# Small tail copies and differences moved from VectorE to ScalarE and GpSimd in a fused attention and gated-MLP kernel

## The chip, the cores and the metric

The kernel runs on one core of one Trainium2 chip. The metric is the device time of one execution in microseconds (us). The core has five engines that work side by side, each through its own queue in order: TensorE (PE, matrix products and transposes), VectorE (DVE), ScalarE (ACT), GpSimd (POOL) and SyncE (SP, which issues most DMAs).

## The reference

Decayed causal attention with 8 batches, 8 heads, a sequence of 576 and a head size of 64, followed by a gated MLP that mixes along the sequence. All inputs and outputs are float32.

```python
scores = scale * q @ k.T                    # per batch and head, 576 x 576
decay  = cum[..., :, None] - cum[..., None, :]   # cum: running sum of log(clip(f))
attn   = softmax(where(causal, -1e9, scores + decay))
x      = (attn @ v)                         # heads side by side: [8, 576, 512]

h      = maximum(x @ w_in, 0.0)             # 512 -> 1024
u, v   = h[..., :512], h[..., 512:]
v_n    = (v - mean(v)) / sqrt(var(v) + 1e-06)
v_s    = einsum('ts,bsd->btd', w_spatial, v_n) + b_spatial[None, :, None]
out    = (u * v_s) @ w_out                  # 512 -> 512
```

## The kernel before, in words

*Arithmetic.* Most matrix products are made from split numbers: a float32 value a is rounded to a shorter format (`hi`, a copy into a tile of type F32R) and the rest is kept as `lo = a - hi`. A product is then the sum of hi x hi, hi x lo and lo x hi. So nearly every operand costs a rounding copy and a difference on the smaller engines before PE can use it. The first pairs of heads (`P < NQ`, `P < NF`) go in plain float32.

*Tiles.* The sequence of 576 is four blocks of 128 and a tail of 64. The tail is what makes the code uneven: a tile with 64 rows or columns leaves half of an engine's 128 partitions empty, so two tails are put together where that is possible.

*Attention.* There are 32 pairs of heads, four to a batch. For each pair `attention` makes transposed probabilities (`transposes`, evicted from PSUM by `evac`: ACT's copy to `eh` at L309, DVE's difference to `el` at L310), the next pair's scores (`scores`: DVE's pass L264 out of PSUM, ACT's exponential L266, POOL's normalisation L274), and the products with v (`attend`: ACT's copy to `xh` at L368, DVE's passes to `xl` at L369 and L371). At the end of a pair, L411 copies the 64 tail columns of `xl` to columns 576 to 639 of `xh`, so that one later product handles the tail's hi and lo together.

*The MLP.* `moe(b)` works on one batch. It makes v for five sequence tiles (four of 128 and the tail), takes statistics (L452, L453, L454, L455), normalises (L456), rounds to `th` (named vnh, ACT, L458), and takes the difference (POOL, L460). For the tail tile, L463 copies the rounded value also into `vb_` (named vb), and L464 writes the difference to partitions 64 to 127 of `th`; both run on DVE. Then it makes u (evicted at L479), and, in two halves of the sequence (256 and 320 columns), the spatial sums; L501 multiplies them by u in place (`g`), L504 rounds `g` to `gh`, and L505 takes the difference `gl`. In the second half the last 64 columns are the tail: L508 copies them from `gh` and `gl` to `gt`, which collects the tails of two batches, so that one `w_out_tile` of 128 rows serves both. `w_out_tile` multiplies by w_out and stores the result. L529 evicts the product to `o` and L531 issues the store.

*Buffers.* PSUM holds two score buffers, two for transposes, two for the MLP, and one each for x0 and x1. The tag U has nine buffers, which hold the eight u tiles and the gl tiles in turn; `gh` has the tag GH, vnh five buffers of its own.

*Order.* `attention` and `moe` are generators that are stepped alternately, by rough PE times (`yield` values), so that attention runs a batch and a quarter ahead of the MLP. In what order the instructions of one engine are finally issued is set by a planner at build time, which simulates a timeline with a cost model (`schedule_with_timeline_sim=True`) and picks ready instructions. At run time each engine follows its list in order and waits on semaphores. The weights are decoded from 64-bit floats on chip at the start (L141 to L151), which loads DVE, ACT and POOL in the first 140 us.

Of the kernel before, what the change touches and what calls it, by code (L numbers as in the profile page):

```python
# [13 lines left out]
ALU = mybir.AluOpType  # L14
# [8 lines left out]
S = 576  # L23
D = 64
NB = 4
TL = 512
# [7 lines left out]
def f32(ap):  # L34
    return ap.bitcast(F32)
# [3 lines left out]
def attn_gmlp_kernel(ctx: ExitStack, tc: tile.TileContext, qk, v, f, w_in, w_sp, b_sp, w_out, out):  # L39
# [17 lines left out]
    V, A, G, T, SY = nc.vector, nc.scalar, nc.gpsimd, nc.tensor, nc.sync  # L57
# [35 lines left out]
    def decay_rows():  # L93
        ft = wk.tile([64, S], F32, name="ft", tag="vt")
        SY.dma_start(out=ft, in_=f)
        ones = wk.tile([64, S], F32, name="ones", tag="xl", bufs=5)
        V.memset(ones, 1.0)
        r0 = cst.tile([64, 2, QK], F32, name="r0", tag="el")
        decay_consts(r0[:], 1)
        V.tensor_scalar(out=ft, in0=ft, scalar1=1.0e-4, scalar2=1.0, op0=ALU.max, op1=ALU.min)  # L100
        A.activation(ft, ft, AF.Ln)
        A.activation(lnc[0:1, 2:3], ft[0:1, 0:1], AF.Exp)
        V.tensor_tensor_scan(out=r0[:, 0, 640:QK], data0=ones, data1=ft, initial=0.0, op0=ALU.mult, op1=ALU.add)
        queries_rows(r0[:], 1, V.tensor_copy, A.copy)
        return r0
# [88 lines left out]
    vb_ = cst.tile([66, DM], F32R, name="vb")  # L194
    G.memset(f32(vb_[64:66, :]), 1.0)

    def mm(o, l, r, st, sp):
        T.matmul(o, l, r, start=st, stop=sp)  # L198
# [177 lines left out]
    def attention(b, ws=None):  # L376
        for P in range(b * PPB, (b + 1) * PPB):
            if P == 0:
                r0s.append(decay_rows())
                for h in range(2):  # L380
                    prep(0, h)

                warm = ps_a.tile([128, 512], F32, name="x0")
                for _ in range(26):
                    mm(warm, zm[:, 0:128], zm[:, 0:512], True, True)
                split_rows(ws, r0s[0])
                split(1)
                yield from scores(0, 0)
                yield from scores_tail(0)
                yield from scores(0, 1)  # L390
            nxt = P + 1 < NPAIR
            prep_v(P)
            if nxt:
                prep(P + 1, 0)
                prep(P + 1, 1)
            yield from transposes(P, 0)
            if nxt:
                yield from scores(P + 1, 0)
            yield from transposes_tail(P)
            if P + 2 < NPAIR:  # L400
                split(P + 2)
            if nxt:
                yield from scores_tail(P + 1)
            xh = wk.tile([128, 640], F32R, name="xh", tag="xh", bufs=5)
            xl = wk.tile([128, S], F32R, name="xl", tag="xl", bufs=5)
            yield from attend(P, 0, xh, xl)
            yield from transposes(P, 1)
            if nxt:
                yield from scores(P + 1, 1)
            yield from attend(P, 1, xh, xl)  # L410
            V.tensor_copy(xh[:, S:640], f32(xl[:, TL:S]))  # L411
            xs[P] = (xh, xl)

    gt = {}
# [9 lines left out]
    def moe(b):  # L424
        X = [xs.pop(b * PPB + p) for p in range(PPB)]
        vh, vl = [], []
        for i in range(NB + 1):
            ps = acc(b)
            n = 0
            for p in range(PPB):  # L430
                xh, xl = X[p]
                if i < NB:
                    t = slice(128 * i, 128 * i + 128)
                    terms = ((xh[:, t], winh), (xh[:, t], winl), (xl[:, t], winh))
                else:
                    terms = ((xh[:, TL:640], winh), (xh[:, TL:640], winl))
                for l, r in terms:
                    mm(ps, l, r[:, p, DM:2 * DM], n == 0, n == len(terms) * PPB - 1)
                    n += 1
                yield 648  # L440
            th = mo.tile([128, DM], F32R, name="vnh", tag="vnh", bufs=5)
            tlo = mo.tile([128, DM], F32R, name="vnl", tag="vnl", bufs=4) if i < NB else None
            x = mo.tile([128, DM], F32, name="vx", tag="vx", bufs=2)
            st = mo.tile([128, 6], F32, name="st", tag="st", bufs=2)
            mv = mo.tile([128, 2], F32, name="mv", tag="mv", bufs=2)
            m = slice(0, 128)
            if i == NB:
                m = slice(0, 64)
                A.copy(x[64:128, :], ps[64:128, :])
                V.tensor_tensor(out=x[m, :], in0=ps[m, :], in1=x[64:128, :], op=ALU.add)  # L450
            A.activation(x[m, :], ps if i < NB else x[m, :], AF.Relu)
            V.bn_stats(out=st[m, :], in_=x[m, :])  # L452
            V.bn_aggr(out=mv[m, :], in_=st[m, :])  # L453
            G.tensor_tensor(out=mv[m, 1:2], in0=mv[m, 1:2], in1=lnc[m, 0:1], op=ALU.add)  # L454
            G.tensor_tensor(out=mv[m, 1:2], in0=mv[m, 1:2], in1=lnc[m, 1:2], op=ALU.pow)  # L455
            V.tensor_scalar(out=x[m, :], in0=x[m, :], scalar1=mv[m, 0:1], scalar2=mv[m, 1:2],  # L456
                            op0=ALU.subtract, op1=ALU.mult)
            A.copy(th[m, :], x[m, :])  # L458
            if i < NB:
                G.tensor_tensor(out=tlo, in0=x, in1=f32(th[:]), op=ALU.subtract)  # L460
                vl.append(tlo)
            else:
                V.tensor_copy(vb_[m, :], f32(th[m, :]))  # L463
                V.tensor_tensor(out=th[64:128, :], in0=x[m, :], in1=f32(th[m, :]), op=ALU.subtract)  # L464
            vh.append(th)
            yield 0
        us = {}
        for j in range(NJ):
            for t0, nt in HALVES:
                ps = acc(b)  # L470
                n = 0
                for p in range(PPB):
                    xh, xl = X[p]
                    for l, r in ((winh, xh), (winl, xh), (winh, xl)):
                        mm(ps[:, 0:nt], l[:, p, 128 * j:128 * j + 128], r[:, t0:t0 + nt], n == 0, n == 3 * PPB - 1)
                        n += 1
                    yield 369
                us[j, t0] = mo.tile([128, 320], F32, name="u", tag="U", bufs=9)
                A.activation(us[j, t0][:, 0:nt], ps[:, 0:nt], AF.Relu)  # L479
        if b == 0:  # L480
            for n in range(8):
                load_rest(n, wo_v, woh, wol, 'GH', 3)
        if b % 2 == 0:
            gt[0] = [mo.tile([128, NJ, 128], F32R, name=f"gt{r}", tag=f"gt{r}") for r in range(2)]
        r0 = 64 * (b % 2)
        for t0, nt in HALVES:
            gh, gl = [], []
            for j in range(NJ):
                ps = acc(b)
                o = ps[:, 0:nt]  # L490
                js = slice(128 * j, 128 * j + 128)
                for c in range(NB):
                    mm(o, vh[c][:, js], sph[:, c, t0:t0 + nt], c == 0, False)
                    mm(o, vh[c][:, js], spl[:, c, t0:t0 + nt], False, False)
                    mm(o, vl[c][:, js], sph[:, c, t0:t0 + nt], False, False)
                    yield 370
                mm(o, vh[NB][:, js], spta[:, t0:t0 + nt], False, False)
                mm(o, vb_[:, js], sptb[:, t0:t0 + nt], False, True)
                yield 246
                g = us[j, t0][:, 0:nt]  # L500
                V.tensor_tensor(out=g, in0=o, in1=g, op=ALU.mult)  # L501
                gh.append(mo.tile([128, 320], F32R, name="gh", tag="GH", bufs=3))
                gl.append(mo.tile([128, 320], F32R, name="gl", tag="U", bufs=9))
                A.copy(gh[j][:, 0:nt], g)  # L504
                G.tensor_tensor(out=gl[j][:, 0:nt], in0=g, in1=f32(gh[j][:, 0:nt]), op=ALU.subtract)  # L505
                if t0:
                    for r, gg in enumerate((gh[j], gl[j])):
                        V.tensor_copy(gt[0][r][:, j, r0:r0 + 64], f32(gg[:, 256:320]))  # L508
            for c0 in (0, 128):
                yield from w_out_tile(b, [g[:, c0:c0 + 128] for g in gh], [g[:, c0:c0 + 128] for g in gl],  # L510
                                      [(b, t0 + c0, 0, 128)])
        if b % 2 == 1:
            yield from w_out_tile(b, *[[g[:, j, :] for j in range(NJ)] for g in gt[0]],
                                  [(b - 1, TL, 0, 64), (b, TL, 64, 64)])
# [98 lines left out]
```

## Time and profile before

| | |
|---|---|
| median of 3 runs | 826.72 us (823.64 to 827.42) |
| the profiled execution | 826.3 us, span 824.5 us |
| mean granted clock of TensorE | 0.973 |
| PE busy | 797.7 us, 97% |
| PEld (weight loads) busy | 711.0 us, 86% |
| DVE busy | 606.8 us, 74% |
| ACT busy | 524.2 us, 64% |
| POOL busy | 467.4 us, 57% |
| DMA, mean | 126 GB/s |

Busy times are shares of the span. A row of the profile's groups reads: line, engine, operation, result <- inputs by the program's names, shapes, count | busy us, mean ns of one | idle time of the engine just before them, and whom it waited for. "Idle before" in a timeline row, in square brackets, is the same for one instruction. PE's records are pipelined: a busy PE is not a PE at its peak. The chain is the work that ended last, followed back from the last instruction to what released it, step by step.

### The profile page before, as it was taken

The page shows a single profiled execution, that of the slowest core. Times are in us where ns is not written, and L with a number is a line of the kernel's source. Part 1 is how long each engine was busy: PE and PEld are TensorE (multiplying, and loading weights), DVE is VectorE, ACT ScalarE, POOL GpSimd, SP SyncE. Part 2 cuts the span into 40 slices and gives each one's busy share as a digit, 9 for nine tenths or more (in the row PEclk, how much of TensorE's full clock was granted, in tenths as well). Part 3 has the DMA queues.
Part 4 walks back from the last instruction along what each step waited for, and adds up shares of the span by engine and source line. Part 5 has one row for each costly group of instructions (what it writes and reads, how often), then busy time and mean ns, then how long its engine had stood idle before and what let it go on. Part 6 is the DMA issues. An engine that isn't in the chain of part 4 may idle for free.

```text
span 824.5 us, 15502 instructions
## 1 busy us (share of the span) xinstructions
PE 797.7 (97%) x4980; PEld 711.0 (86%) x4980; DVE 606.8 (74%) x1838; ACT 524.2 (64%) x1360; POOL 467.4 (57%) x637
## 2 busy tenths in 40 slices
PE   7999997999999999999999999999999999999997
PEld 4676776998799989989899889999899988999896
DVE  5879899767886868777797678868697767866431
ACT  5576766655686667576676576766676757754431
POOL 5758787444665537355675446556664547543131
PEclk8697998999999999999999999999999999999999
DMA  7446863555555565555645465455634664430001
GB/s 205 134 131 179 206 140 96 137 149 141 125 133 124 139 144 124 131 149 133 151 124 129 117 165 137 117 140 142 165 77 114 162 169 115 98 78 12 26 1 65
DMA packets 47475, 103.50 MB, mean 126 GB/s; under 512 B 6961, under 2 KB 15153, under 8 KB 47330
## 3 DMA queue, kind: packets, MB, share of 16 engines
q1 hardware_dynamic: 47074, 101.98, 49.4%
q8 instruction: 40, 0.66, 0.3%
q10 hardware_dynamic: 320, 0.52, 0.3%
q14 instruction: 41, 0.34, 0.1%
HBM read 39.41 MB, written 10.68 MB: 61 GB/s over the span
## 4 chain that ended last, share of the span: by engine, by line
PE 79%; DVE 9%; DMA 5%; POOL 2%; ACT 2%; issue 1%; SPq 0%; POOLq 0%; DVEq 0%; ACTq 0%
PE ps L198 42%; PE sc L198 15%; PE x L198 11%; PE tp L320 7%; PE tp L198 2%; PE tp L333 2%; DMA out_dram<-o 2%; DMA w<-in_dram 1%; DVE tt L264 1%; POOL tt L274 1%; DVE vx L456 1%; DVE el L310 1%; DMA tb<-lo 1%; DVE wa L148 1%; DVE xh L411 1%
## 5 line engine op out<-in xcount | busy, mean ns | idle before, releaser
L274 POOL TENSOR_SCALAR tt<-tt,sm 128x128 f32<-128x128 f32 (+3 forms) x256 | 140.3, 566 | 119.3 <-DVE sm L270 83.1
L264 DVE CUSTOM_DVE_ANT_0 tt<-sc,zm 128x128 f32<-128x128 f32 (+3 forms) x256 | 122.7, 485 | 69.0 <-PE tp L320 53.6
L266 ACT ACTIVATE tt<-tt,nm 128x128 f32<-128x128 f32 (+3 forms) x256 | 144.3, 564 | 41.4 <-DVE nm L264 36.1
L309 ACT CAST eh<-tp 128x512 fp32r<-128x512 f32 (+1 forms) x270 | 111.8, 425 | 79.4 <-PE tp L320 46.2
L310 DVE TENSOR_TENSOR el<-tp,eh 128x512 fp32r<-128x512 f32 (+1 forms) x270 | 128.1, 484 | 22.0 <-ACT eh L309 20.0
L320 PE MATMUL tp<-ident,tt 128*128 128x128 f32 x640 | 114.7, 282 | 2.7 <-DVE el L310 2.2
L198 PE MATMUL sc<-ta 128*128 128x128 f32 (+1 forms) x336 | 109.8, 332 | 6.8 <-DVE nm L264 6.1
L198 PE MATMUL sc<-tb 68*128 68x128 f32 (+1 forms) x336 | 105.8, 319 | 0.3 <-DMA tb<-lo 0.3
L198 PE MATMUL x<-eh,vt 128*128 128x320 f32 (+4 forms) x378 | 104.0, 286 | 1.5 <-POOL vt L243 0.9
L505 POOL TENSOR_TENSOR gl<-u,gh 128x256 fp32r<-128x256 f32 (+1 forms) x64 | 51.7, 809 | 90.3 <-ACT gh L504 89.2
L198 PE MATMUL x<-el,vt 128*128 128x256 f32 x324 | 92.6, 306 | 0.0
L212 POOL TENSOR_TENSOR lo<-raw,hi 128x640 fp32r<-128x640 f32 (+1 forms) x56 | 83.0, 1503 | 12.5 <-ACT hi L210 11.9
L320 PEld LDWEIGHTS tp<-ident,tt 128*128 128x128 f32 x640 | 77.9, 144 | 13.6 <-issue 2.4
L198 PEld LDWEIGHTS sc<-ta 128*128 128x128 f32 x336 | 64.2, 191 | 14.6 <-DVE nm L264 9.2
L198 PEld LDWEIGHTS x<-eh,vt 128*128 128x128 f32 x378 | 71.6, 190 | 4.7 <-POOL vt L243 1.3
L198 PE MATMUL ps<-sph,vnh 128*128 128x256 f32 (+1 forms) x240 | 72.5, 302 | 2.1 <-ACT o L529 2.1
L198 PE MATMUL ps<-xh,winh 128*128 128x256 f32 (+1 forms) x232 | 70.8, 305 | 1.2 <-ACT u L479 1.2
L368 ACT CAST xh<-x 64x256 fp32r<-64x256 f32 (+1 forms) x128 | 49.9, 393 | 34.4 <-PE x L198 32.5
L198 PE MATMUL ps<-sph,vnl 128*128 128x256 f32 (+1 forms) x240 | 71.5, 298 | 0.0
L198 PE MATMUL ps<-spl,vnh 128*128 128x256 f32 (+1 forms) x240 | 71.2, 297 | 0.0
L198 PE MATMUL ps<-xl,winh 128*128 128x256 f32 (+1 forms) x232 | 69.1, 298 | 0.0
L198 PE MATMUL ps<-xh,winl 128*128 128x256 f32 (+1 forms) x232 | 69.0, 297 | 0.0
(190 smaller groups left out, 2145.6 us busy)
## 6 DMA issues: line engine op xcount, KB each, us to landing
raw<-in_dram SPq DMA_DIRECT2D x28, 608.0 KB
ta<-hi SPq DMA_DIRECT2D x56, 304.0 KB
vraw<-in_dram SPq DMA_DIRECT2D x32, 320.0 KB
tb<-hi SPq DMA_DIRECT2D x56, 160.0 KB
ta<-lo SPq DMA_DIRECT2D x56, 160.0 KB
out_dram<-o SPq DMA_DIRECT2D x32, 256.0 KB
ta<-hi SPq DMA_DIRECT2D x56, 144.0 KB
tb<-lo SPq DMA_DIRECT2D x56, 144.0 KB
```

What stands on the lines that cost most here:

```text
L148: V.scalar_tensor_tensor(out=af, in0=lo, scalar=2.0 ** -52, in1=af, op0=ALU.mult, op1=ALU.mult)
L198: T.matmul(o, l, r, start=st, stop=sp)
L212: G.tensor_tensor(out=lo[:, c], in0=raw[:, c], in1=f32(hi[:, c]), op=ALU.subtract)
L264: V.tensor_tensor_reduce(out=t, in0=sc[:, 0:n], in1=zm[:, 640 - n:640], scale=-0.125, scalar=3.0e38, op0=ALU.add, op1=ALU.min, accum_out=n ...
L266: last["exp", P, h, i] = A.activation(t, t, AF.Exp, bias=nm[:, i:i + 1], scale=-1.0, accum_out=sm[:, i:i + 1])
L274: G.tensor_scalar(out=t, in0=t, scalar1=sm[:, i:i + 1], scalar2=1.0, op0=ALU.mult, op1=ALU.mult)
L309: A.copy(h_ap, ps)
L310: V.tensor_tensor(out=l_ap, in0=ps, in1=f32(h_ap), op=ALU.subtract)
L320: T.transpose(out=tp[:, (i - c) * 128:(i - c + 1) * 128], in_=tt[h][:, TOFF[i] + 128 * c:TOFF[i] + 128 * c + 128], identity=ident)
L333: T.transpose(out=tp[:, j * 128:(j + 1) * 128], in_=tl[:, c * 128:(c + 1) * 128], identity=ident)
L368: last[P, h] = A.copy(hi, ps[m0:m0 + 64, 0:n])
L505: G.tensor_tensor(out=gl[j][:, 0:nt], in0=g, in1=f32(gh[j][:, 0:nt]), op=ALU.subtract)
```

## The change

Three places move off DVE.

1. L411, the copy of x's tail (32 times), is issued on ACT.
2. For the tail tile of the normalised v (8 times), the copy into `vb_` is made by ACT, straight from the unrounded `x` instead of from the rounded `th`; the difference into partitions 64 to 127 of `th` is made by POOL.
3. In the second half of the gating (32 times), `gh` and `gl` hold 256 columns only. The 64 tail columns are rounded by ACT straight from `g` into `gt[0]`, and POOL takes their difference straight into the other tile. The two DVE copies at L508 are gone, and L504 and L505 shrink from 320 to 256 columns there.

```diff
             yield from attend(P, 1, xh, xl)
-            V.tensor_copy(xh[:, S:640], f32(xl[:, TL:S]))
+            A.copy(xh[:, S:640], f32(xl[:, TL:S]))
             xs[P] = (xh, xl)
...
             else:
-                V.tensor_copy(vb_[m, :], f32(th[m, :]))
-                V.tensor_tensor(out=th[64:128, :], in0=x[m, :], in1=f32(th[m, :]), op=ALU.subtract)
+                A.copy(vb_[m, :], x[m, :])
+                G.tensor_tensor(out=th[64:128, :], in0=x[m, :], in1=f32(th[m, :]), op=ALU.subtract)
             vh.append(th)
...
-                A.copy(gh[j][:, 0:nt], g)
-                G.tensor_tensor(out=gl[j][:, 0:nt], in0=g, in1=f32(gh[j][:, 0:nt]), op=ALU.subtract)
+                A.copy(gh[j][:, 0:256], g[:, 0:256])
+                G.tensor_tensor(out=gl[j][:, 0:256], in0=g[:, 0:256], in1=f32(gh[j][:, 0:256]), op=ALU.subtract)
                 if t0:
-                    for r, gg in enumerate((gh[j], gl[j])):
-                        V.tensor_copy(gt[0][r][:, j, r0:r0 + 64], f32(gg[:, 256:320]))
+                    th, tlo = (gt[0][r][:, j, r0:r0 + 64] for r in range(2))
+                    A.copy(th, g[:, 256:320])
+                    G.tensor_tensor(out=tlo, in0=g[:, 256:320], in1=f32(th), op=ALU.subtract)
             for c0 in (0, 128):
```

Here `V` is DVE, `A` is ACT and `G` is POOL. PE's instructions, the DMAs and the buffers stay as they are.

## The prediction, made before the result was known

> **What bounds the kernel now.** I read the page's busy times first, then the windows by stage, then what TensorE (PE) waited for, and last what stood on the vector engine (DVE) ahead of those waits. In the window rows the columns are stretch, length, and then busy time and instruction count of PE, PEld, DVE, ACT and POOL.
>
> ```profile
> PE 797.7 (97%) x4980; PEld 711.0 (86%) x4980; DVE 606.8 (74%) x1838; ACT 524.2 (64%) x1360; POOL 467.4 (57%) x637
> ...
> 0.00:140.00 140.00, 127.66 (x560) 91.53 (x561) 116.26 (x343) 90.14 (x235) 104.39 (x138) 0.87 0.61 160
> 140.00:200.00 60.00, 60.00 (x402) 57.11 (x402) 42.45 (x141) 37.59 (x102) 32.05 (x44) 0.95 0.54 135
> 200.00:780.00 580.00, 570.74 (x3775) 526.11 (x3774) 435.53 (x1326) 383.53 (x998) 317.16 (x438) 1.00 0.50 124
> ```
>
> From 140 us on PE is full: 60.00 of 60, then 570.74 of 580 us at a granted clock of 1.00. All that another engine can give back between 200 and 780 us is 580 - 570.74 = 9.3 us. Before 140 us PE is idle for 12.3 us, and DVE, with 116.26 of 140 us, is the busiest of the other engines. The waits of PE, first for 120 to 200 us and then for 200 to 780 us (total us, times, longest):
>
> ```profile
> PE sc L198 <- DVE nm L264: 3.9, 2, 3.1
> ...
> PE ps L198 <- ACT o L529: 2.9, 5, 1.1
> PE sc L198 <- DVE nm L264: 2.2, 4, 0.7
> PE tp L320 <- DVE el L310: 2.0, 4, 0.7
> ```
>
> So in the long middle DVE costs PE 4.2 us and ACT 2.9 us. The change takes work off an engine that is not the bound there. It is worth what it removes from these few waits, and from the opening stage.
>
> **The change part by part.** The edits touch these groups (count, busy us, mean ns; then idle time of the engine before them). L411 is the copy of the tail of x. L508 is the pair of copies of the gated tails, L504 and L505 the rounding and the difference ahead of them. L463 and L464 are the normalised tail's copy and difference. L458 and L460 are the nearest rows for what replaces those two.
>
> ```profile
> L460 POOL TENSOR_TENSOR vnl<-vx,vnh 128x512 fp32r<-128x512 f32 x32 | 41.7, 1313 | 18.9 <-ACT vnh L458 18.7
> ...
> L505 POOL TENSOR_TENSOR gl<-u,gh 128x320 fp32r<-128x320 f32 x32 | 28.1, 880 | 58.4 <-ACT gh L504 58.4
> ...
> L505 POOL TENSOR_TENSOR gl<-u,gh 128x256 fp32r<-128x256 f32 x32 | 23.6, 738 | 32.0 <-ACT gh L504 30.8 <-DVE sm L292 0.7
> ...
> L411 DVE CAST xh<-xl 128x64 fp32r<-128x64 f32 x32 | 16.2, 508 | 0.1
> ...
> L508 DVE CAST gt<-gh 128x64 fp32r<-128x64 f32 x32 | 14.8, 464 | 15.2 <-ACT gh L504 15.1
> L504 ACT CAST gh<-u 128x320 fp32r<-128x320 f32 x32 | 14.7, 458 | 19.1 <-DVE u L501 5.9 <-PE sc L198 5.2 <-issue 4.5
> ...
> L504 ACT CAST gh<-u 128x256 fp32r<-128x256 f32 x32 | 12.8, 405 | 12.8 <-DVE u L501 8.5 <-PE sc L198 2.3 <-issue 1.8
> ...
> L508 DVE CAST gt<-gl 128x64 fp32r<-128x64 f32 x32 | 8.1, 252 | 3.7 <-POOL gl L505 3.1
> ...
> L464 DVE TENSOR_TENSOR vnh<-vx,vnh 64x512 fp32r<-64x512 f32 x8 | 5.8, 721 | 0.2
> ...
> L463 DVE CAST vb<-vnh 64x512 fp32r<-64x512 f32 x8 | 5.3, 658 | 1.3 <-ACT vnh L458 1.3
> ...
> L458 ACT CAST vnh<-vx 64x512 fp32r<-64x512 f32 x8 | 5.0, 620 | 3.2 <-DVE vx L456 3.0
> ```
>
> *Removed from DVE:* 16.2 + 14.8 + 8.1 + 5.3 + 5.8 = 50.2 us of busy time, and up to 15.2 + 3.7 us in which DVE stood idle at L508 with other work queued behind it.
>
> *Added to ACT.* Between 256 and 320 columns L504 grows by 53 ns, 0.83 ns a column, so 192 ns are fixed and 64 columns take 192 + 53 = 245 ns, by extrapolation. The ends are the fixed part, 0.19, and the 256 columns' 0.405. I take 0.245, which rests on the same operation in the same place. L411 becomes 32 x 0.245 = 7.8 us, the tails of gh another 7.8, the copy into vb 8 x 0.62 = 5.0, and the shortened L504 gives 32 x 0.053 = 1.7 back: +18.9 us in all.
>
> *Added to POOL.* L505 grows by 142 ns over 64 columns, so 738 - 4 x 142 = 170 ns are fixed and a 64-column difference takes 170 + 142 ns, 0.31 us (ends 0.17 and 0.738): 32 x 0.31 = 9.9 us, less 32 x 0.142 = 4.5. The moved L464 is priced by L460's 512 columns, 8 x 1.31 = 10.5 us. It writes partitions 64 to 127 from inputs on 0 to 63, which no POOL row of this trace does; the ends are DVE's 0.72 and twice 1.31. Sum: +15.9 us on POOL.
>
> **What reaches the end: L411.** It has one row that matters more than its mean (min, median, max ns), and one place that shows why:
>
> ```profile
> L411 DVE CAST xh<-xl x32: 176/380/1539, 48.7 to 777.6; 128x64 fp32r<-128x64 f32 x32
> ...
> 516.65 1.57 POOL L243 TENSOR_TENSOR vt<-vraw,vt 128x640 fp32r<-128x640 f32 x1
> ...
> 517.01 1.26 DVE L411 CAST xh<-xl 128x64 fp32r<-128x64 f32 x1
> ...
> 518.19 0.54 DVE L264 CUSTOM_DVE_ANT_0 tt<-sc,zm 128x384 f32<-128x384 f32 x1
> ...
> 518.80 0.40 PE L198 MATMUL sc<-ta 128*128 128x288 f32 x1 [0.61 <-DVE nm L264]
> ```
>
> A copy that can take 0.18 us took 1.26, ending when POOL's 1.57 us instruction ended at 518.22. L264, the first pass over the next scores, stood behind it, and PE idled 0.61 us for a free score buffer. The same order (L411 long on DVE, then the late L264 or L310, then an idle PE) stands ahead of four more waits:
>
> ```profile
> 209.47 0.74 DVE L411 CAST xh<-xl 128x64 fp32r<-128x64 f32 x1
> ...
> 210.96 0.41 PE L320 MATMUL tp<-ident,tt 128*128 128x128 f32 x2 [0.36 <-DVE el L310]
> ...
> 304.23 0.61 DVE L411 CAST xh<-xl 128x64 fp32r<-128x64 f32 x1
> ...
> 306.06 0.40 PE L198 MATMUL sc<-ta 128*128 128x288 f32 x1 [0.17 <-DVE nm L264]
> ...
> 330.72 1.10 DVE L411 CAST xh<-xl 128x64 fp32r<-128x64 f32 x1
> ...
> 332.35 0.40 PE L198 MATMUL sc<-ta 128*128 128x288 f32 x1 [0.69 <-DVE nm L264]
> ...
> 613.68 1.11 DVE L411 CAST xh<-xl 128x64 fp32r<-128x64 f32 x1
> ...
> 615.32 0.40 PE L198 MATMUL sc<-ta 128*128 128x288 f32 x1 [0.70 <-DVE nm L264]
> ```
>
> That is 0.61 + 0.36 + 0.17 + 0.69 + 0.70 = 2.5 us of the 4.2 in which PE waits for DVE. I take all of it as gained: in each of the five L411 lasts longer than its shortest 0.18 us by more than PE's idle time. Late next in these places is nothing that PE shows; it is full on both sides.
>
> In the opening stage L411 lies on the chain that ended last four times (start, us on the chain); the last row is a window of L411 alone (busy us, count):
>
> ```profile
> 67.18 0.07 DVE xh L411
> ...
> 89.45 0.64 DVE xh L411
> ...
> 101.18 0.10 DVE xh L411
> ...
> 131.99 0.10 DVE xh L411
> ...
> 0.00:140.00 140.00, 3.06 (x5) 0.87 0.61 160
> ```
>
> Together 0.9 us, which I also take. The ends are 0, if the next DVE instruction meets the same POOL instruction, and the 3.1 us that L411 lasts there in all.
>
> *L508, L463, L464.* No wait of PE stands behind them in the rows above, so I cost their removal at nothing. The cover is PE's own queue: the tile of w_out that reads gt comes once in two batches, and the spatial sums read vb last. If that cover is gone, the price is ACT's 0.245 and POOL's 0.31 us on 16 and 8 occasions, under 4 us together. On the other side, POOL's difference waits for ACT's rounding just ahead of it, but L505 itself lies between, 0.738 us against 0.245, so nothing new is waited for. The buffer of g is read for 0.31 us longer; the next gl takes one of the same nine, eight of which hold u. None of the moved instructions issues a DMA.
>
> *The new wait.* On ACT the copy of x's tail waits for DVE's last pass over xl. Queued behind it are the evictions L309 and the exponentials L266, and behind those PE's transposes and scores. Its longest form is the chain of the two DVE passes:
>
> ```profile
> L369 DVE TENSOR_TENSOR xl<-x,xh 64x320 fp32r<-64x320 f32 x64 | 31.0, 485 | 6.9 <-ACT xh L368 5.9
> ...
> L371 DVE TENSOR_TENSOR xl<-x,xl 64x320 fp32r<-64x320 f32 x54 | 26.4, 488 | 1.6
> ```
>
> 0.485 + 0.488 = 0.97 us, if ACT has nothing else to do in between; 0 if it has. PE feels at most a part: L411 on DVE reached it in 5 of the 27 cases that lie behind the opening. I take one wait of 0.5 us, and 2.9 x 18.9/383.5 = 0.15 us more of the waits that ACT already causes: +0.65 us. The ends are 0 and 32 x 0.97 = 31 us.
>
> **One rule weighed.** The row at 517.01 shows a DVE copy held until a POOL instruction ends. [...]
>
> ```profile
> L456 DVE TENSOR_SCALAR vx<-vx,mv x40: 523/546/2316, 106.8 to 791.9; 128x512 f32<-128x512 f32 x32, 64x512 f32<-64x512 f32 x8
> ```
>
> Of L456 the trace shows a shortest 0.52 and a longest 2.32 us. If three of its 40 are held for the difference of 1.8 us more (15.9 of 467.4 us is 3% more POOL time, so this is generous), and one in five reaches PE as with L411, the sum would rise by 1.1 us. I leave that out of the sum and in the range.
>
> **The sum.** -2.5 - 0.9 + 0.65 = -2.8 us. The profiled execution took 826.3 us (span 824.5, with 1.8 around it), so 823.5. The three runs have a median of 826.72, 0.4 above the profiled one; on that footing the forecast is 823.9 us. About 0.5%, 4.1 us, is what a measurement here tells from no change: the forecast lies inside.
>
> **The rivals.**
>
> *It changes nothing* (20%). PE is full for 97% of the span, and a gap that closes may open at the next dependence: 826 us, give or take 1.5. For it speaks that PE's work is untouched; against it, that L411 stands behind five waits.
>
> *A new order gains more* (22%). The order of instructions on each engine comes from a planner that simulates a timeline, so moving 104 instructions to other engines can reorder everything after the first. In the opening PE loses 12.3 us, of which a single wait for nm takes 3.1 (the row for 120 to 200 us). If that one goes too, and another 1 us of the 4.2, the time is 823.9 - 4.1 = 819.8. Against it: a new order can lose as well, and only 0.10 us of L411 stands on the chain after 102 us.
>
> *ACT's new wait decides* (12%, slower). ACT is strictly in order. If of 32 waits for xl one in four reaches PE with 0.97 us, that is 7.8 us against the 3.4 gained: 826.72 + 4.4 = 831.1. It turns slower than before from the fourth such wait on (4 x 0.97 = 3.9). For it speaks that L411 on DVE reached PE in 5 of 27 cases; against it that ACT is idle for 34% of the middle stage, while DVE idles for 25%.
>
> *POOL becomes late* (6%, slower). [...] As a mechanism here: each batch puts a 1.31 us difference in front of the normalisations L274, which PE's transposes need. If all eight reach PE, 10.5 - 3.4 = +7.1: 833.8. Against it stands that POOL is busy for 317.16 of 580 us.
>
> **How the numbers follow.** The forecast's case, 821 to 826 us, has 40%; of that a third lies below 822.6. Faster: 22% and 13%, with 2% of the second case's spread: 0.37. Slower by over 4.1 us (above 830.9): 6% of POOL's case, 9% of ACT's and 2% for a bad new order: 0.17. The rest, 0.46, is no change that can be told. The range leaves out a tenth on either side: 816.5 from a new order that gains twice as much as said, 832.0 from ACT's case just past its price.
>
> **What would show it.** Right: L411 on ACT at about 0.25 us; DVE near 557 us, ACT near 543, POOL near 483; the five waits gone, and PE's waits on DVE between 200 and 780 us below 2.5 us. The step on ACT is wrong if the new L411 has idle time before it put down to DVE's xl, and PE then waits for eh or for tt. The step on POOL is wrong if PE waits for vnh's tail, or for tt put down to L274. The whole is wrong if PE's order differs so much that its busy time or its idle time before 140 us moves by more than 3 us; then the planner, and not the moved copies, sets the result.

## The result, and the profile after

The changed kernel takes 813.23 us in the median of 4 runs (813.18 to 813.83), against 827.07 us for the kernel before. The ratio is 0.983 (95% interval 0.981 to 0.986): 13.8 us faster, where 2.8 were forecast, and outside the forecast range.

The page after, first part, then the same windows by stage and the waits of PE for 225 to 763 us (columns as before):

```profile
PE 788.3 (97%) x4980; PEld 704.9 (87%) x4980; DVE 567.1 (70%) x1726; ACT 535.2 (66%) x1432; POOL 478.1 (59%) x677
...
0.00:140.00 140.00, 127.06 (x591) 92.33 (x592) 115.86 (x342) 92.88 (x247) 103.20 (x139) 0.91 0.60 160
140.00:200.00 60.00, 58.95 (x399) 54.95 (x398) 42.78 (x137) 39.22 (x109) 32.56 (x48) 1.00 0.58 144
200.00:767.00 567.00, 563.19 (x3749) 521.66 (x3748) 398.57 (x1229) 389.32 (x1045) 326.38 (x468) 1.00 0.51 125
```

```profile
PE x L198 <- POOL vt L243: 1.8, 2, 0.9
PE x L198 <- DVE eh L342: 0.8, 2, 0.4
PE sc L198 <- DVE nm L264: 0.5, 3, 0.2
PE ps L198 <- ACT o L530: 0.2, 1, 0.2
```

The 1.8 us of waits for POOL's vt (L243) are new in this stretch. They stand also in the experiments e7 and e8 below, in which POOL got no work, so POOL's added work alone doesn't explain them. PE is as full as it was, and the span is still 13.0 us shorter. To see where, I take the end of a pair of heads (its last ACT copy L368) as a milestone in both traces. The fifth pair ends at 128.5 us before and 129.4 after; the ninth at 232.4 and 225.4; the last at 775.9 and 762.6. So nothing is gained up to the fifth pair, 7.9 us from there to the ninth, and 6.3 us in the long middle. The middle in the two traces, before and then after:

```profile
232.40:775.90 543.50, 536.21 (x3564) 495.65 (x3563) 406.57 (x1240) 359.30 (x937) 297.06 (x406) 1.00 0.50 124
```

```profile
225.40:762.60 537.20, 533.65 (x3564) 495.36 (x3563) 373.49 (x1158) 367.30 (x990) 306.42 (x436) 1.00 0.51 126
```

The same 3564 matrix products take 6.3 us less; 3.7 of that is idle time of PE (7.3 us before, 3.55 after), and 2.6 us lie inside records that count as busy. The granted clock is the column behind POOL's. Two windows of before, and the same two of after:

```profile
73.90:84.10 10.20, 9.95 (x26) 6.36 (x25) 7.70 (x31) 6.47 (x19) 8.46 (x10) 0.50 1.00 253
138.80:145.60 6.80, 6.30 (x28) 6.29 (x29) 5.00 (x17) 3.70 (x10) 4.87 (x7) 0.50 0.25 51
```

```profile
73.90:84.10 10.20, 8.66 (x41) 5.32 (x39) 9.21 (x33) 7.72 (x24) 9.48 (x14) 1.00 0.84 233
138.80:145.60 6.80, 6.80 (x52) 6.64 (x51) 6.46 (x17) 3.60 (x12) 6.28 (x9) 1.00 0.86 189
```

Before, PE ran at half clock for 6.8 us from 138.8 us on, beginning in the idle gap of 3.1 us that ends at 139.30. In that stretch the 128x256 products started 0.213 us apart (eight steps from 140.43 to 142.13 us), at full clock 0.118 (eleven from 129.54 to 130.84). At this ratio PE's 6.30 busy us there did the work of 3.5, so 2.8 us of clock were lost, by estimate. After, the clock stays at 1.00 in both windows. From the fifth to the ninth pair the idle time of PE fell by 3.2 us (97.49 of 103.9 us busy before, 92.74 of 96.0 after), and with the 2.8 us of clock that is 6.0 of the 7.9 us, in this one execution of each.

The instruction that made this gap is none of the moved ones:

```profile
135.25 3.52 DVE L148 SCALAR_TENSOR_TENSOR wa<-w,wa 128x256 f32<-128x256 uint32 x1
135.60 2.89 POOL L212 TENSOR_TENSOR lo<-raw,hi 128x640 fp32r<-128x640 f32 x2
138.69 0.55 DVE L264 CUSTOM_DVE_ANT_0 tt<-sc,zm 128x384 f32<-128x384 f32 x1
...
139.30 0.61 PE L198 MATMUL sc<-ta 128*128 128x288 f32 x1 [3.12 <-DVE nm L264]
```

L148 belongs to the decoding of the weights. Its shortest time is 0.40 us; here it lasted 3.52 us, to 138.77, and POOL's two passes ran to 138.49. In the changed kernel none of the 20 lasts over 1.64 us; they stand elsewhere among DVE's and POOL's instructions. So what was gained at this place came from a new order and not from a moved copy.

Half-clock time can't simply be added to idle time, though. In experiment e8 below a gap of 3.03 us (105.5 to 108.5 us) had no half clock behind it, and neither had one of 1.83 us in the changed kernel (ending at 132.2); in experiment m3 a gap of 1.82 us (ending at 131.7) was followed by 3.4 us of it. The 10.2 us of half clock from 73.9 us on are gone in the changed kernel, and the fifth pair ends no earlier. And over the executions of the kernel before that were timed beside the experiments, the mean clock goes from 0.971 to 0.983, which is 10 us of clock (0.012 of 826), while the time goes from 828.5 us (mean of the four at 0.971) to 825.6 us (of the three at 0.983).

The moved instructions cost what was forecast (count | busy us, mean ns | idle before):

```profile
L464 POOL TENSOR_TENSOR vnh<-vx,vnh 64x512 fp32r<-64x512 f32 x8 | 10.6, 1325 | 4.0 <-ACT vnh L458 3.5 <-PE ps L198 0.3
L509 POOL TENSOR_TENSOR gt<-u,gt 128x64 fp32r<-128x64 f32 x32 | 10.1, 325 | 1.2 <-ACT gt L508 1.2
L411 ACT CAST xh<-xl 128x64 fp32r<-128x64 f32 x32 | 7.9, 246 | 0.0
L508 ACT CAST gt<-u 128x64 fp32r<-128x64 f32 x32 | 7.8, 243 | 4.6 <-DVE u L501 4.6
L463 ACT CAST vb<-vx 64x512 fp32r<-64x512 f32 x8 | 4.9, 618 | 0.0
```

246 ns against 245, 325 against 312, 1325 against 1313, 618 against 620. L411 never made ACT wait (0.0).

### The profile page after: what moved, and what is told of

Same layout as the page of the kernel before. It is cut to its first block, busy times and chain, and to the rows that moved or that the text cites. A ratio compares the mean times of both kernels' runs of the same rounds, so it can differ in the third digit from the quotient of the medians.

```text
span 811.5 us, 15566 instructions
## 1 busy us (share of the span) xinstructions
PE 788.3 (97%) x4980; PEld 704.9 (87%) x4980; DVE 567.1 (70%) x1726; ACT 535.2 (66%) x1432; POOL 478.1 (59%) x677
## 4 chain that ended last, share of the span: by engine, by line
PE 87%; DVE 5%; POOL 2%; ACT 2%; DMA 2%; issue 1%; SPq 0%; ACTq 0%; POOLq 0%; DVEq 0%
PE ps L198 47%; PE sc L198 16%; PE x L198 12%; PE tp L320 8%; PE tp L198 2%; PE tp L333 2%; DMA out_dram<-o 1%; POOL tt L274 1%; DVE w L145 1%; ACT tt L266 1%; DVE tt L264 1%; DVE eh L342 0%; DVE wa L142 0%; DVE ef L305 0%; DMA w<-in_dram 0%
## 5 line engine op out<-in xcount | busy, mean ns | idle before, releaser
L274 POOL TENSOR_SCALAR tt<-tt,sm 128x128 f32<-128x128 f32 (+3 forms) x256 | 138.3, 558 | 94.7 <-DVE sm L270 86.4
L310 DVE TENSOR_TENSOR el<-tp,eh 128x512 fp32r<-128x512 f32 (+1 forms) x270 | 127.9, 485 | 25.0 <-ACT eh L309 22.8
L198 PE MATMUL sc<-ta 128*128 128x128 f32 (+1 forms) x336 | 107.8, 327 | 3.9 <-DVE nm L264 3.8
L505 POOL TENSOR_TENSOR gl<-u,gh 128x256 fp32r<-128x256 f32 x64 | 47.2, 738 | 79.3 <-ACT gh L504 76.1
L368 ACT CAST xh<-x 64x256 fp32r<-64x256 f32 (+1 forms) x128 | 49.8, 392 | 28.4 <-PE x L198 26.9
```

The source lines that it names most:

```text
L274: G.tensor_scalar(out=t, in0=t, scalar1=sm[:, i:i + 1], scalar2=1.0, op0=ALU.mult, op1=ALU.mult)
L310: V.tensor_tensor(out=l_ap, in0=ps, in1=f32(h_ap), op=ALU.subtract)
L368: last[P, h] = A.copy(hi, ps[m0:m0 + 64, 0:n])
L505: G.tensor_tensor(out=gl[j][:, 0:256], in0=g[:, 0:256], in1=f32(gh[j][:, 0:256]), op=ALU.subtract)
```

## The experiments

The theories. **A**: a DVE copy that is held while POOL works stood on PE's path, and each part of the change is worth its own holds. **B**: the planner's new order of the instructions did it, above all in the opening with its half clock. **C**: the held instructions stand in one queue at the same places, so that the parts pay only together.

All results in one table. "To 9th" is the time of the ninth pair's end, "middle" from there to the last pair's end, "idle" PE's idle time in the middle, all from the one profiled execution of each kernel; the ratio is from its timed runs against the kernel before.

| kernel | ratio (95% interval) | to 9th, us | middle, us | idle, us |
|---|---|---|---|---|
| before | 1 | 232.4 | 543.5 | 7.3 |
| n1, planning constant | 1.0006 (0.9987 to 1.0026) | 232.4 | 543.9 | 7.8 |
| n2, evictions swapped | 0.9966 (0.9947 to 0.9984) | 230.8 | 543.6 | 8.8 |
| m1, pace of loading | 0.9993 (0.9977 to 1.0009) | 231.1 | 543.9 | 7.8 |
| e1, L411 alone | 0.9936 (0.9899 to 0.9973) | 229.3 | 542.6 | 7.0 |
| e2, normalised tail alone | 0.9967 (0.9947 to 0.9988) | 231.9 | 540.5 | 6.3 |
| e3, gated tails alone | 1.0004 (0.9987 to 1.0022) | 232.1 | 544.4 | 7.7 |
| e4, all but L411 | 0.9983 (0.9965 to 1.0001) | 230.3 | 541.6 | 7.4 |
| e5, all but the normalised tail | 0.9880 (0.9865 to 0.9894) | 226.8 | 540.2 | 4.8 |
| e6, all but the gated tails | 0.9852 (0.9833 to 0.9871) | 226.1 | 538.2 | 4.6 |
| the change | 0.9832 (0.9805 to 0.9859) | 225.4 | 537.1 | 3.5 |
| n4, the change, evictions swapped | 0.9902 (0.9871 to 0.9933) | 233.3 | 538.4 | 4.6 |
| m2, the change, pace of loading | 0.9851 (0.9825 to 0.9878) | 228.6 | 537.8 | 4.2 |
| m3, the change, planning constant | 0.9837 (0.9814 to 0.9860) | 225.9 | 537.8 | 4.1 |
| d1, the change and a spare DVE copy | 0.9971 (0.9953 to 0.9989) | 228.8 | 543.5 | 7.8 |
| e7, DVE copies as additions | 0.9946 (0.9926 to 0.9965) | 232.4 | 538.1 | 5.0 |
| e8, L411 on DVE out of PSUM | 0.9957 (0.9931 to 0.9984) | 230.6 | 542.7 | 7.0 |
| b1, the change and L342 on ACT | 0.9836 (0.9805 to 0.9868) | 225.6 | 536.7 | 3.1 |

(n4's profiled execution took 822.5 us, 5 us over its median of 817.3, so its 233.3 is on the long side. e4's, 822.7 us, is the fastest of its ten, 3.2 us under their median, so its figures are on the short side.)

**The parts, one by one, and one neutral edit.** Each kernel takes one of the diff's three edits; n1 changes `t_attn, t_moe = 36000.0, 51000.0` to `36300.0, 51000.0` and nothing else.

> Only the copy of x's tail (L411, 32 times) goes to ACT; the rest is as before. Theory A (DVE copies held behind POOL instructions stood on PE's path): L411 was ahead of five PE waits of 2.5 us in all in the middle, so the ratio to before is about 0.995 to 0.991, with those five waits gone. Theory B (a new order of the planner, and with it where PE's clock falls to half in the opening): the result has no relation to L411's own price; it may be anything from 0.98 to 1.01, and what differs is PE's idle time and the half-clock time before 240 us (17 us of half clock between 73 and 146 us in before, none there in the changed kernel).

> Only the normalised tail's copy and difference (8 times) go to ACT and POOL. Theory A: DVE loses 11 us of work that stood behind no PE wait, so ratio 0.997 to 1.000. Theory B: the order changes at the first batch's tail near 140 us, beside the gap of 3.1 us and the half clock of 6.8 us that follow it; if those go, the ratio is 0.990 to 0.994 although DVE's load hardly changes.

> Only the gated tails are split straight into their tiles by ACT and POOL. Theory A: 23 us leave DVE and 19 us of its idle time at L508 can go, but no PE wait stands behind them, so ratio 0.996 to 1.000. Theory B: the order can change from the first gated tail on only (about 180 us), so everything before 180 us, the gap at 139 us and both half-clock stretches included, stays as it was; ratio 0.995 to 1.003.

> The kernel before, with one planning constant changed from 36000 to 36300: no instruction is added, removed or moved to another engine, and only the order on the engines differs. Theory A: ratio 0.998 to 1.002. Theory B: the time moves by 3 us or more in either direction, with the half-clock time in the opening and PE's idle time as the parts that differ.

The three parts alone give 0.64%, 0.33% and nothing: 0.9% together, where the change gives 1.7%. So the parts do not simply add up (theory A). n1 says nothing on B: in its trace PE, DVE, ACT and POOL have the same instructions in the same sequence as before (by operation, names and shapes), although its expectation took the order to differ. L411 alone gains 6.3 us between the fifth and the ninth pair and 0.9 us in the middle, though the waits behind L411 are gone there; it loses 3.2 us up to the fifth pair (131.7 us against 128.5), in another order. (Orders are compared in the traces: the longest common sequence of PE's matrix products by operation, names and shapes. Up to the ninth pair it is 866 of 1146 here.) At a batch's tail the next held instruction takes the place of L411. DVE, POOL and PE in e1's timeline:

```profile
605.85 1.56 POOL L243 TENSOR_TENSOR vt<-vraw,vt 128x640 fp32r<-128x640 f32 x1
605.91 1.78 DVE L456 TENSOR_SCALAR vx<-vx,mv 64x512 f32<-64x512 f32 x1 [0.88 <-POOL mv L455]
...
607.62 1.14 DVE L310 TENSOR_TENSOR el<-tp,eh 128x512 fp32r<-128x512 f32 x2
608.44 0.41 PE L320 MATMUL tp<-ident,tt 128*128 128x128 f32 x2 [0.70 <-DVE el L310]
```

L456, 0.52 us where it runs free, is held for 1.78 us, L310 is late, and PE idles 0.70 us. In e2 it is the other way round: L463 is off DVE, and L411 still stands there with 1.11 us ahead of a PE wait of the same length.

```profile
705.99 1.11 DVE L411 CAST xh<-xl 128x64 fp32r<-128x64 f32 x1
707.01 0.55 DVE L264 CUSTOM_DVE_ANT_0 tt<-sc,zm 128x384 f32<-128x384 f32 x1
...
707.62 0.40 PE L198 MATMUL sc<-ta 128*128 128x288 f32 x1 [0.70 <-DVE nm L264]
```

**The change without one part.** Each takes one of the three edits back.

> The changed kernel with the copy of x's tail (L411) back on DVE. Theory A (held DVE copies, each part by itself): the sum of the two single parts run alone, 0.9967 and 1.0004, so about 0.997. Theory C (the copies stand in one DVE queue at the same places, so that the parts only pay together): clearly less than the full change's 0.983, and L411 again ahead of PE's waits at the batches' tails; 0.990 to 0.997. Theory B (order and clock in the opening): the result goes by whether PE's clock falls to half between 60 and 150 us; with no such stretch 0.988 or less.

> The changed kernel with the normalised tail's copy and difference back on DVE. Theory A: the sum of the single parts, 0.9936 and 1.0004: 0.994. Theory C: between that and the full change's 0.983. Theory B: as in the full change if the opening has no half-clock stretch after 60 us, since the order there is set by L411's move: 0.985 to 0.988.

> The changed kernel with the gated tails as before (rounded over 320 columns, copied by DVE). The part alone gave 1.0004. Theory A: 0.9903, the sum of the other two. Theory C: 0.986 to 0.990. Theory B: the opening up to 180 us is that of the full change, so its gain of about 7 us there (0.991) is kept, and what is missing to 0.983 is in the middle.

Without L411's move almost all is lost: 0.998. So L411 is worth 1.5% where the other two edits are in, and 0.6% alone. The normalised tail is worth 0.5% in company and 0.3% alone; the gated tails 0.2% in company, which the intervals do not separate from nothing, and nothing alone. That is the direction of C, but not proof of it: A's 0.997 for e4 lies inside the measured interval, e4 and e6 lie just outside the ranges that C gave them, and 3.2 us of L411's smaller worth alone were lost before the fifth pair, in another order. B asked 0.985 to 0.988 of e5 if its opening had no half clock after 60 us. It has two stretches of 3.4 us there (from 84.7 and 132.5 us), so its 0.988 does not test B.

The clearest pair is e4 and the change, because in the middle they run in the same order: 3527 of 3561 matrix products stand in the same sequence, and so do nearly all of DVE's instructions, L411 aside. With L411 on DVE the middle takes 541.6 us, without it 537.1. One place in e4, then the same place in the change:

```profile
705.18 2.93 POOL L212 TENSOR_TENSOR lo<-raw,hi 128x640 fp32r<-128x640 f32 x2 [0.81 <-ACT hi L210]
...
705.68 1.11 DVE L411 CAST xh<-xl 128x64 fp32r<-128x64 f32 x1
...
706.72 0.54 DVE L264 CUSTOM_DVE_ANT_0 tt<-sc,zm 128x384 f32<-128x384 f32 x1
...
707.33 0.40 PE L198 MATMUL sc<-ta 128*128 128x288 f32 x1 [0.70 <-DVE nm L264]
```

```profile
696.69 2.95 POOL L212 TENSOR_TENSOR lo<-raw,hi 128x640 fp32r<-128x640 f32 x2 [0.81 <-ACT hi L210]
...
697.18 0.55 DVE L264 CUSTOM_DVE_ANT_0 tt<-sc,zm 128x384 f32<-128x384 f32 x1
...
697.87 0.23 ACT L411 CAST xh<-xl 128x64 fp32r<-128x64 f32 x1
...
697.96 0.35 PE L198 MATMUL sc<-ta 128*128 128x288 f32 x1
```

Five such waits, 0.70 + 0.36 + 0.69 + 0.35 + 0.70 = 2.8 us, stand behind a long L411 in e4 and are gone in the change. The waits for `o` are 1.2 us in e4 and 0.2 in the change. That is nearly all of the 3.9 us of idle time between the two (7.4 and 3.5); the other 0.6 of the 4.5 us lie inside records that count as busy.

The middle can be taken apart in this order, since e2, e4, e6 and the change share it (at least 3500 matrix products in the same sequence), while before and the change have 2518 in common. From before to e2, the normalised tail's move and with it the new order, the middle falls by 3.0 us; from e2 to e6, L411's move, by 2.3; from e6 to the change, the gated tails, by 1.0. In four executions with the very order of the change the middle is 537.1 to 538.4 us, so the last step is no larger than that scatter.

**Is it the holding, or the load on DVE?** e7 keeps the three copies on DVE and makes each an addition of zeros; e8 makes only x's tail on DVE, from PSUM.

```diff
-            V.tensor_copy(xh[:, S:640], f32(xl[:, TL:S]))
+            V.tensor_tensor(out=xh[:, S:640], in0=f32(xl[:, TL:S]), in1=zm[:, 0:64], op=ALU.add)   # e7
...
+            if s0:                                                                                 # e8
+                tail, part = ps[l0:l0 + 64, 256:320], xl[m0:m0 + 64, TL:S]
...
+                V.tensor_tensor(out=xh[m0:m0 + 64, S:640], in0=tail, in1=f32(part), op=...)
```

> The kernel before, with the three kinds of DVE copies (L411, L463, L508) still on DVE, but each issued as an addition of a tile of zeros (two inputs) in place of a copy (one input); L464 stays on DVE. ACT and POOL get nothing. If the copies are slow because a one-input copy is held until a running POOL instruction ends, and the additions are not, L411 falls from 508 ns to about 0.2 us in the mean and L508 likewise, and then theory A (holding is what costs) gives most of the change's gain, ratio 0.983 to 0.990; if the load moved off DVE is what counts, 0.995 to 1.000. If the additions are held as well, their means stay near 0.5 us and the ratio near 1.

> The kernel before, but the tail columns of xh are made by DVE straight out of PSUM (two additions or differences of 64 partitions per pair, one input in PSUM) in place of the copy L411 out of SBUF. DVE's count grows by 32, ACT and POOL get nothing. Passes with an input in PSUM (L369, L371) never lasted over 496 ns in the profile of before, whatever POOL did, so if it is the holding of L411 that costs, the 64 new ones take about 0.2 us each, never over 0.3, and the ratio is like that of moving L411 to ACT alone, 0.990 to 0.996. If what counts is the load on DVE, the ratio is 1.000 (14 us of DVE work in place of 16). If it is the planner's order alone, anything from 0.985 to 1.005.

Two rows, e7's addition out of SBUF and e8's out of PSUM (min, median, max ns):

```profile
L411 DVE TENSOR_TENSOR xh<-xl,zm x32: 205/432/1586, 48.9 to 772.2; 128x64 fp32r<-128x64 f32 x32
```

```profile
L374 DVE TENSOR_TENSOR xh<-x,xl x54: 217/222/229, 151.7 to 773.8; 64x64 fp32r<-64x64 f32 x54
```

The addition with both inputs in SBUF is held like the copy, up to 1586 ns; of the 54 with an input in PSUM none took over 229 ns, and of the other 10 in e8 none over 224. In e8 DVE does 14.1 us of work on x's tail (54 x 222 and 10 x 212 ns) in place of 16.2, ACT and POOL get nothing, and the ratio is that of moving L411 to ACT, 0.996 and 0.994, with intervals that overlap; the middle is the same too, 542.7 and 542.6. That fits the holding and not the load; but the two run the middle in different orders (2363 products in the same sequence), so it is no proof. e7 speaks against holding as a measure by itself. Its ratio had to stay near 1 if the additions were held, and did not: in the middle its 23 L411 take 17.0 us in place of 11.9, yet the middle fell to 538.1 us, with no work moved off DVE. The planner gave it an order of its own (2394 products in sequence with before), and its L463 takes 845 ns at most, against 1208; how the 5 us divide between the two stays open.

**A copy that nothing waits for.** The changed kernel, and the old copy once more, into a tile that nobody reads.

```diff
             A.copy(xh[:, S:640], f32(xl[:, TL:S]))
+            V.tensor_copy(spare[:], f32(xl[:, TL:S]))
```

> The changed kernel with the removed DVE copy of x's tail made once more, 32 times, by DVE into a tile that nothing reads; ACT's copy stays, so no data waits for DVE's. It costs DVE at most 32 x 0.18 = 5.9 us of work where nothing holds it. If holding is what costs, the copies last 0.5 us in the mean again, PE's idle time after 225 us rises by 2 us or more, and the ratio to before goes from 0.983 to 0.988 to 0.995. If it was that x's tail came late, or chance of order, it stays at 0.981 to 0.986, as the changed kernel did under two of three changes of order.

824.35 us: with the spare copy 11 of the 13.8 us are lost, more than the expectation had (0.997 against 0.988 to 0.995). The middle, and the copy's times:

```profile
228.80:772.30 543.50, 535.69 (x3561) 495.24 (x3560) 390.68 (x1179) 368.69 (x989) 306.72 (x436) 1.00 0.50 124
```

```profile
L413 DVE COPY spare<-xl x32: 175/330/1794, 48.3 to 774.1; 128x64 f32<-128x64 f32 x32
```

The middle is back at 543.5 us, as before, and PE's idle time at 7.8 (7.3 before, 3.5 in the change). At one place the picture of the prediction returns as it was:

```profile
513.94 1.57 POOL L243 TENSOR_TENSOR vt<-vraw,vt 128x640 fp32r<-128x640 f32 x1
...
514.30 1.26 DVE L413 COPY spare<-xl 128x64 f32<-128x64 f32 x1
...
516.09 0.40 PE L198 MATMUL sc<-ta 128*128 128x288 f32 x1 [0.61 <-DVE nm L264]
```

PE's waits in the middle:

```profile
PE ps L198 <- ACT o L532: 2.7, 3, 1.8
PE sc L198 <- DVE nm L264: 2.3, 5, 0.7
PE tp L320 <- DVE el L310: 1.3, 1, 1.3
```

The waits for ACT's `o`, which no edit touches, were 2.6 us before and 0.2 in the change, and are 2.7 here. They do not simply go with the held copy: they are 2.6 in e1, with L411 on ACT, and 0.2 in e2, with L411 held on DVE. And the planner reordered the middle for the spare copy (2558 products in the change's sequence), so the 11 us are the price of the copy, its 16.9 us on DVE, and that order together.

**How much is order?** Four edits that move no work: n2 and n4 start the alternation of the first evictions at 1 (`nev = [1]`), m1 and m2 change `step(wgen, dw, 4500.0)` to `5000.0`, m3 is n1's edit in the changed kernel.

> The kernel before, with ACT and DVE swapped in the alternation by which the first pairs' transposes are evicted (the counter starts at 1): the same work, another order from 28 us on. If the order in the opening sets the changed kernel's gain between 129 and 232 us (7.9 of 13 us: a gap of 3.1 us at 139 us and the half clock behind it), this one may lose or win some 5 us against before there, ratio 0.988 to 1.006; if only the held copies count, that gap stays and the ratio is 0.998 to 1.002.

> The changed kernel with the same swap in the opening. If its gain was a lucky order in the opening, about 8 us of it can go: ratio to before 0.983 to 0.995. If the gain is tied to the moved copies, it stays: 0.981 to 0.986.

> The kernel before, with the pace at which the weights' loading is stepped beside the first batch's attention changed from 4500 to 5000: 55 lines of order differ on PE, all in the opening, and no work is moved. If order in the opening is worth several us, the time moves by 2 us or more; if the opening of before is as good as its order can be without moving the copies, 0.998 to 1.002.

> The changed kernel with the same change of pace, and again 55 lines of order. If the changed kernel's opening owes part of its gain to a lucky order, the ratio to before rises to 0.986 to 0.992, as it did when the alternation of the evictions was swapped (0.990); if the gain is tied to the copies, 0.981 to 0.985.

> The changed kernel with the planning constant 36300 in place of 36000, the edit that left the kernel before at 1.0006. Same two expectations: 0.986 to 0.992 if the order in the opening was luck, 0.981 to 0.985 if not.

Only the swapped evictions changed an order. With n1, m1, m2 and m3 the four engines have the same sequence as their parent over the whole span (by operation, names and shapes); the 55 lines that m1's and m2's expectations speak of do not show in it. Their times are repetitions, and agree with their parents' to 2.2 us in the median.

n4 reorders the opening alone. Its ratio, 0.990, is where its expectation put a lucky order: by medians 4.0 us of the gain are lost, and in the profile most of the loss lies up to the ninth pair. n2 reorders both stretches and gains 2.6 us. Between the two kernels with swapped evictions the change is worth 7.2 us (824.5 to 817.3), between the two as given 13.8. So about half of the 13.8 us, 6.6, comes with this order of the opening (theory B in part). Some of the opening is tied to L411 in every order tried: from the fifth to the ninth pair the eight kernels that copy x's tail on DVE out of SBUF take 101.1 to 103.9 us, d1 99.0, and those that do not, b2 aside, 95.6 to 98.2. How much of that is the copy and how much its order was not tested.

In the middle n2, with the copies on DVE in another order, takes 543.6 us. But e7's 538.1 with nothing moved off DVE shows that an order can be worth several us there too, unless the additions themselves are.

**Three more steps on the same path.** Moving the last tail copy on DVE (L342) to ACT; moving L456 to POOL; 40 warm-up products in place of 26.

```diff
-                V.tensor_copy(ET["h"][64:128, :, S:640], f32(ET["l"][64:128, :, S:640]))
+                A.copy(ET["h"][64:128, :, S:640], f32(ET["l"][64:128, :, S:640]))            # b1
...
-            V.tensor_scalar(out=x[m, :], in0=x[m, :], scalar1=mv[m, 0:1], scalar2=mv[m, 1:2],
+            G.tensor_scalar(out=x[m, :], in0=x[m, :], scalar1=mv[m, 0:1], scalar2=mv[m, 1:2],   # b2
...
-                for _ in range(26):
+                for _ in range(40):                                                          # b3
```

> The changed kernel, and the one DVE copy of a tail that it still has (L342, 27 times, the tail of eh) on ACT as well. In the changed kernel PE waited for L342 at 401.76 and 588.42 us (0.36 and 0.40 us), and L342 takes 373 ns in the mean on DVE against 225 ns where no POOL instruction runs. If a held copy on DVE costs PE as L411 did, the ratio to before falls from 0.983 to 0.978 to 0.982; if what is left is hidden, it stays at 0.983; ACT gets 27 x 0.3 = 8 us more.

> The changed kernel with one more DVE pass out of and into SBUF moved: the normalisation L456 (40 times, 0.52 us where nothing holds it, up to 1.8 us in the changed kernel) goes to POOL, at about 0.75 us each by L274's rows, +29 us of POOL time. If holding by POOL is what costs, taking the longest held instruction off DVE gains 1 to 4 us more (ratio 0.979 to 0.982); if POOL's extra 29 us hold the other DVE passes or come late themselves, 0.984 to 0.990.

> The changed kernel with 40 instead of 26 idle matrix products at the start. Both kernels run PE at half clock from about 12 to 36 us (23.9 us, so some 12 us lost), after a pause of PE near 10 to 13 us. If the longer warm-up bridges that pause and the clock stays up, the time falls by 5 to 12 us (ratio 0.969 to 0.977). If the products only delay the first scores, by up to 14 x 0.216 = 3 us, the ratio is 0.983 to 0.988.

b1 takes 812.54 us (0.984, 0.981 to 0.987): PE's 0.8 us of waits for L342 go, which the runs can't tell from the change alone. b2 takes 856.58 us (1.036, 1.033 to 1.038), slower than before and far outside both expectations: on POOL L456 costs 2.07 us, not 0.75.

```profile
L456 POOL TENSOR_SCALAR vx<-vx,mv x40: 2065/2074/2174, 109.9 to 819.4; 128x512 f32<-128x512 f32 x32, 64x512 f32<-64x512 f32 x8
```

That is 83 us of POOL time and not 29, and PE waits for vnh from L464 and L458 and for the late scores. So taking held work off DVE is not a gain by itself. b3 takes 816.18 us (0.986, 0.983 to 0.990): the first scores come later, and the half clock is only put off, to 18.0 us:

```profile
12.40:18.00 5.60, 3.58 (x15) 1.62 (x12) 5.53 (x14) 1.84 (x5) 1.58 (x1) 1.00 0.92 205
18.00:38.50 20.50, 20.50 (x51) 14.27 (x52) 14.96 (x48) 11.29 (x32) 14.38 (x15) 0.50 0.26 85
```

No version tried beats the change by more than the runs can tell.

## Why the prediction was wrong

- **What bounds the kernel** held: PE is at 97% after as before, and what was gained came from PE's waits and the opening.
- **The prices of the moved instructions** held, all within 5%.
- **The step that failed is the sum itself: it had two terms for what was taken away, both for L411, and none for the rest.** L411 was put at 2.5 us in the middle and 0.9 in the opening, everything else at nothing. Measured were 6.3 us in the middle, 7.0 up to the ninth pair.
- **L411 in the middle** was the right mechanism, with a size that was right or too small, by the order and by what else is off DVE. In one and the same order its move is worth 4.5 us (e4 and the change), of which 2.8 are waits directly behind it, as the prediction summed them; with the gated copies still on DVE it is worth 2.3 (e2 and e6). What the sum left out are 1.0 us of waits for `o` and 0.6 us inside records that count as busy.
- **L411 in the opening** at 0.9 us was the largest miss. Whenever L411 left DVE, the planner reordered the opening. The longest gap there, 3.1 us, came from L148, held for 3.52 us, which no edit touches and which stands elsewhere in the new order. How much of the opening is left to the copy stays open.
- **L463 and L464 at nothing** failed. "No wait of PE stands behind them" was read row by row, while L456, L411, L463 and L464 stand in one queue at each batch's tail. Their move is worth 3.0 us in the middle alone, with the new order that came with it, and 0.5% in company (817.4 us without it, 813.2 with it).
- **L508 at nothing** held: 0.2%, which the intervals do not separate from nothing.
- **The new wait on ACT,** 0.65 us and the price of a rival, did not come: the new L411 has 0.0 us of idle time before it. PE never waited for POOL's part of the tail either. DVE's L456, for which the prediction kept 1.1 us in its range, was not held more beside POOL's added work: its 40 took 28.6 us in all, after 29.6.
- **"A new order gains more"** was the nearest rival (819.8 us), and it named the gap of 3.1 us; the longest in that stretch of the changed kernel is 1.8. The prediction's last sign points the same way: PE's busy time moved by 9.4 us, over the 3 that were to mean that the planner sets the result. The runs bear that out for part of the opening and, in the middle, for the part of the 3.0 us that the new order brought; L411 is worth its 2.3 to 4.5 us there in a fixed order. The count of moved instructions was wrong as well: 112 left DVE, not 104.

## What to carry to other kernels

Before comparing two versions of a planned kernel, compare the sequence of instructions on each engine. A variant whose edit also reorders the rest prices both at once, and a "neutral" edit that leaves the sequence as it was only repeats the measurement. The pair to read is the one with the same sequence and one instruction moved. And list all instructions that are held in one queue, also those that the change does not touch: the longest gap here came from one of them.

## What the runs showed of the hardware

- Some DVE instructions with all operands in SBUF were held while POOL worked: 64 columns took 175 to 1794 ns as a copy (d1) and 205 to 1586 ns as an addition of two SBUF inputs (e7), but 217 to 229 ns with one input in PSUM (e8, on 64 partitions). At 517.01 us in the kernel before and 514.30 us in d1 the copy ended 0.05 us after POOL's instruction. Beside two POOL passes in a row, 2.89 us together, L148 lasted 3.52 us and ended 0.28 us after them. Not every such instruction was held: at 122.39 us in the kernel before L148 took 0.41 us, while POOL's L460 ran from 122.27 to 123.93 us.
- On ACT the same 64 columns took 231 to 265 ns in the changed kernel (L411, 32 times).
- ACT did not take a ready instruction ahead of a waiting one: in the kernel before it stood idle for 0.54 us until L458 could start at 118.51 us, and L305, next in its queue, started at 119.04 us, though the transposes that L305 evicts had ended by 117.33 us.
- On POOL a pass over 128x512 that subtracts and then multiplies by two columns took 2.07 us (b2), one that multiplies by a column and by 1.0 took 0.72 us (L274, before).
- In the changed kernel PE's clock fell to half for 23.9 us from 12.4 us on though PE was busy for 22.6 of them, and 14 more warm-up products moved this to 18.0 us and 20.5 us of length (b3) without removing it. Later half-clock stretches lasted 3.4 us (e5, m3), 6.8 and 10.2 us (before). A gap of 1.83 us in the changed kernel and one of 3.03 us in e8 had none behind them.
- At half clock the 128x256 products started 0.213 us apart, at full clock 0.118 (before, from 140.43 and from 129.54 us).
